# A kernel whose order comes from a list of jobs: GpSimd jobs tied to the vector job ahead of them, new durations in the list, and transposed rows offered later

## The chip, the cores and the metric

The kernel runs on one core of a Trainium2 chip, as one program. The metric is the device time of one execution in microseconds (us), median of three runs. The engines are TensorE (PE; its weight loads PEld), VectorE (DVE), ScalarE (ACT), GpSimd (POOL) and SyncE (SP, which here issues the DMAs). Each runs its own instructions in the order in which the program lists them, and waits for the others through semaphores.

## The reference

Attention over 4 batches, 12 heads, 448 positions and head size 64, in float32, and then two feed-forward layers on the 1792 rows of 768:

```
q_n, k_n = rmsnorm(q, g_q), rmsnorm(k, g_k)        # x / sqrt(mean(x*x) + 1e-6) * g
scores = q_n @ k_n.T / 8;  scores -= rowmax(scores)
attn = exp(scores);  attn /= (rowsum(attn) + 1e-9)
x = heads_joined(attn @ v)                         # [1792, 768]
x = square(relu(x @ w_in)) @ w_out                 # 768 -> 2048 -> 768
g = x @ w_gate
out = (silu(g) * (x @ w_val)) @ w_out2             # 768 -> 1536 -> 768
```

## The kernel before

Attention works on 24 pairs of heads, g = 0 to 23, six to a batch. A pair has 7 tiles of scores (`PT`), 128 rows by 448 each. For a tile PE multiplies (`sc`), DVE takes the negated row maximum and scales it by the query's norm (`maxima`: `sc`, `m`), ACT takes the exponential with the sum of each row (`ring`, `sum`), PE turns the result by four transposes (`pt`), ACT copies that out of PSUM (`turned_p`); when seven are there, PE multiplies with the values (`o`). Products in full precision are made of high and low parts (`kst`, `kst_lo` and so on): the high part is a cast on ACT or DVE, the low part a subtraction on GpSimd or DVE.

The norms come beside that. Squares of the keys and queries (`nat`) are made on ACT or GpSimd, DVE sums them (`ss`), and `rsqrt` makes the inverse root by three Newton steps: for the first pairs all of it on DVE, later the three steps on GpSimd, each a job of four small instructions (`rst`, `rms`). The result for the keys lies in `stage`. `transposed` turns it on PE (`rows` from `stage`), ACT copies it out (`rkr`), and for the first five pairs PE spreads it over the partitions (`rk`) for the scaling of the keys (`kq`). The sums of the exponentials go the same way: `norms` takes their reciprocal on DVE (`sum`), `transposed` turns them (`rows` from `sum`), ACT copies them (`zr`), PE spreads them (`zb`, first five pairs), and they scale `o` into `ox`, from which the input `x` of the first layer is made.

PE has other work only once the list says that the 35th exponential is done (`LEND`): from then on products of the first layer (`h_a`, `ya`, line 325) stand between those of attention. Ahead of it small transposes (`warm`) fill PE's first 20 us. After attention only the two layers are left.

No one writes the order by hand. Each step is a generator that yields jobs, such as `yield {"A": 467, "W": 300}, f`: f may run on ACT for 467 ns or on DVE for 300 ns. "P" is PE, "G" GpSimd, "V" a vector job, and "W" a vector job that takes part in the port described below. A clock of the list's own runs through these durations while the program is built; `dispatch` takes, for each engine that is free on that clock, the ready job of lowest rank and emits its instructions. An engine other than the first named takes a job only when the first is behind by more than a spare time. So the durations decide which engine takes a job and in which order everything stands; the chip then runs each engine's list in that order, with waits only for data. `port` is a time up to which, on the list's clock, neither a GpSimd job nor a "W" job may start: the list never lets them overlap, but nothing holds the chip to that.

Of the kernel before, what the change touches and what calls it, by code (L numbers as in the profile page):

```python
# [14 lines left out]
ALU = mybir.AluOpType  # L15
# [37 lines left out]
X_AT = 3  # L53
X_FLIGHT = 3
PE_SLACK = 500
JOIN_FROM = 6
OUT_ORDER = [2, 3, 4, 5, 0, 1]
DEC_FIRST = 14
# [20 lines left out]
def attention_two_ffn_kernel(  # L79
# [19 lines left out]
    nc = tc.nc  # L99
    PSUM = bass.MemoryType.PSUM  # L100

    def as_f32(ap):
        return ap.bitcast(F32)
# [66 lines left out]
                heapq.heappush(timers, (clock[0] + p, serial[0], t, None))  # L170
            return

    port = [0.0]

    def meant(job):
        e = next(iter(job[1][0]))
# [15 lines left out]
    def dispatch(e):  # L192
        queues[e] = [job for job in queues[e] if not job[3]]
        if not queues[e] or free_at[e] > clock[0]:
            return False
        q = [job for job in queues[e] if e == meant(job) or late(job) > cost(job, e) + spare[e]]
        if port[0] > clock[0]:
            q = [job for job in q if not ported(job, e)]
        if not q:
            return False  # L200
        job = min(q, key=lambda job: (job[0].rank, job[2]))
        job[3] = True
        t, p, _, _ = job
        p[1](engines[e])
        done = free_at[e] = clock[0] + cost(job, e)
        if ported(job, e):
            port[0] = done
        if e == "S":
            dma_free[0] = max(dma_free[0], clock[0] + 1100) + p[2] / DMA_RATE
            done = dma_free[0] + 900  # L210
        else:
            done += p[2] if len(p) > 2 else settle[e]
        heapq.heappush(timers, (done, job[2], t, e))
        return True
# [46 lines left out]
    def load_weights(items):  # L261

        hilo, parts = {}, {}

        def chunk(key, place, c, raw_at):
            name, f = key  # L270
            late = f"{name}{f}_{c}"
            src = w_tiles[name][f] if name in w_tiles else w_rows[name][bass.ts(f, 128), :]
            src = src.bitcast(I32).rearrange("p (n two) -> p n two", two=2)
            raw = raw_at[0].tile([128, WC, 2], I32, tag=raw_at[1], name=f"raw_{late}")
            yield from dma(lambda e: e.dma_start(out=raw, in_=src[:, bass.ts(c, WC), :]), 8 * WC * 128)
            yield lambda: was and not leading
            a_at = was.pop(0)
            a = a_at[0].tile([128, WC], F32, tag=a_at[1], name=f"wa_{late}")
            yield {"A": 413, "W": 269}, lambda e: (
                e.activation(out=a, in_=raw[:, :, 1].bitcast(F32), func=ACTF.Copy, scale=2.0 ** -112)  # L280
                if e is nc.scalar
                else e.tensor_scalar(
                    out=a, in0=raw[:, :, 1].bitcast(F32), scalar1=2.0 ** -112, scalar2=None, op0=ALU.mult
                )
            )
            yield lambda: wts
            t_at = wts.pop(0)
            t = t_at[0].tile([128, WC], F32, tag=t_at[1], name=f"wt_{late}")
            ai, ti = a.bitcast(I32), t.bitcast(I32)
            yield {"W": 269}, lambda e: e.tensor_scalar(  # L290
                out=ti, in0=raw[:, :, 0].bitcast(U32), scalar1=2.0 ** -29, scalar2=7.0, op0=ALU.mult, op1=ALU.min
            )
            raws.append(raw_at)
            yield {"W": 469}, lambda e: e.scalar_tensor_tensor(
                out=ti, in0=ai, scalar=SIGN_BIT, in1=ti, op0=ALU.bitwise_and, op1=ALU.bitwise_or
            )
            yield {"W": 469}, lambda e: e.scalar_tensor_tensor(
                out=ti, in0=ai, scalar=3, in1=ti, op0=ALU.logical_shift_left, op1=ALU.bitwise_or
            )
            was.append(a_at)  # L300
            if c == 0:
                yield lambda: place or free
                pool, hi_tag, lo_tag = placed[key] = place or free.pop(0)
                hilo[key] = tuple(
                    pool.tile([128, DM], F32R, tag=tag, name=f"{part}_{name}{f}")
                    for part, tag in (("hi", hi_tag), ("lo", lo_tag))
                )
                parts[key] = 0
            yield lambda: key in hilo
            hi, lo = (x[:, bass.ts(c, WC)] for x in hilo[key])  # L310
            yield {"A": 413, "W": 269}, lambda e: copy(e, hi, t)
            yield {"W": 469, "G": 956}, lambda e: e.tensor_tensor(out=lo, in0=t, in1=as_f32(hi), op=ALU.subtract)
            wts.append(t_at)
            parts[key] += 1
            if parts[key] == DM // WC:
                wt[key] = hilo[key]

        for key, place, rank in items:
            for c in range(DM // WC):
                yield lambda: raws  # L320
                spawn(chunk(key, place, c, raws.pop(0)), rank + c / 10)
# [123 lines left out]
    def rsqrt(y, ss, t, ends, fused):  # L445

        def begin(e):
            e.tensor_scalar(out=ss, in0=ss, scalar1=1.0 / D, scalar2=EPS_RMS, op0=ALU.mult, op1=ALU.add)
            e.tensor_scalar(
                out=y.bitcast(I32), in0=ss.bitcast(I32), scalar1=-0.5, scalar2=RSQRT_MAGIC, op0=ALU.mult, op1=ALU.add  # L450
            )

        def step(e, to):
            e.tensor_tensor(out=t, in0=y, in1=y, op=ALU.mult)
            if fused:
                e.scalar_tensor_tensor(out=t, in0=t, scalar=-0.5, in1=ss, op0=ALU.mult, op1=ALU.mult)
            else:
                e.tensor_tensor(out=t, in0=t, in1=ss, op=ALU.mult)
                e.tensor_scalar(out=t, in0=t, scalar1=-0.5, scalar2=1.5, op0=ALU.mult, op1=ALU.add)
            for dst, part in to:  # L460
                a, b = (t, y) if part is None else (t[:, part], y[:, part])
                if fused:
                    e.scalar_tensor_tensor(out=dst, in0=a, scalar=1.5, in1=b, op0=ALU.add, op1=ALU.mult)
                else:
                    e.tensor_tensor(out=dst, in0=a, in1=b, op=ALU.mult)

        if fused:
            def all_steps(e):
                begin(e)
                for i in range(3):  # L470
                    step(e, ends if i == 2 else [(y, None)])

            yield {"W": 170 * (10 + len(ends))}, all_steps
            return
        yield {"W": 300}, begin
        for i in range(3):
            yield {"G": 900}, lambda e: step(e, ends if i == 2 else [(y, None)])

    stat, halves = {}, {}
    sum_wide, stage = (  # L480
# [10 lines left out]
    def row_sums(g, w):  # L491

        b, p = divmod(g, PB)
        yield lambda: nat_free
        where = nat_free.pop(0)
        x = tile_at(where, [128, PT * D], F32, f"nat{g}_{w}")
        src = (k_n, q_n)[w][b][:, bass.ts(p, PT * D)]
        yield from dma(lambda e: e.dma_start(out=x, in_=src), 128 * PT * D * 4)
        yield {"A": 467} if g == 0 else {"G": 1091, "A": 467}, lambda e: (
            e.activation(out=x, in_=x, func=ACTF.Square) if e is nc.scalar  # L500
            else e.tensor_tensor(out=x, in0=x, in1=x, op=ALU.mult)
        )
        rows = x.rearrange("p (t d) -> p t d", d=D)
        if g or w:
            yield lambda: (1 if g and Q_HOLD > 1 else 0) in summed
        yield {"V": 535}, lambda e: e.tensor_reduce(out=stat["ss", b][:, w, p], in_=rows, axis=AX.X, op=ALU.add)  # L506
        if where[0] is not xp:
            nat_free.append(where)
        halves[g] = halves.get(g, 0) + 1
# [45 lines left out]
    def spread(rows, parts, name):  # L555
# [9 lines left out]
                    start=True, stop=True,  # L565
                )

        yield {"P": 1100}, broadcast, 0
        return ps, where

    def spread_k(g, rows, r):
# [34 lines left out]

    def transposed(src, dst):

        yield lambda: t_banks
        where = t_banks.pop(0)  # L610
        pt = tile_at(where, [128, 512], F32, "rows")
# [50 lines left out]
    def split(g, x, name, w):  # L662
        yield lambda: g < 2 or scored[0] >= PT * (g - 1)
        hi = ap.tile([128, w], F32R, tag=f"{name}{g % 2}", name=f"{name}{g}")
        lo = ap.tile([128, w], F32R, tag=f"{name}{g % 2}_lo", name=f"{name}_lo{g}")
        yield {"A": 467, "W": 300}, lambda e: copy(e, hi, x)
        yield {"G": 1106, "W": 535}, lambda e: e.tensor_tensor(out=lo, in0=x, in1=as_f32(hi), op=ALU.subtract)
        return [hi, lo]

    def release_kq(g):  # L670
# [4 lines left out]
    def prep_k(g, kr, rk, rk_at):  # L675

        yield lambda: gained
        e = yield {"W": 596, "A": 467}, lambda e: (
            e.activation(out=kr, in_=kr, func=ACTF.Copy, scale=gqk[:, 0:1]) if e is nc.scalar
            else e.scalar_tensor_tensor(out=kr, in0=kr, scalar=gqk[:, 0:1], in1=rk, op0=ALU.mult, op1=ALU.mult)  # L680
        )
# [70 lines left out]
    def softmax(g, tiles, parts, tops, where):  # L752
# [17 lines left out]
                )  # L770
                at += each

        yield {"V": 215 * len(tops) + n * 467}, maxima
        if g not in sums:
            yield lambda: g in sums or sum_free
            if g not in sums:
# [19 lines left out]
    def norms(g):  # L796
# [3 lines left out]
            e.tensor_scalar(out=z, in0=z, scalar1=EPS_SUM, scalar2=None, op0=ALU.add)  # L800
            e.reciprocal(z, z)

        yield {"V": 240}, inverse
        yield lambda: zr_free
        zr_at = zr_free.pop(0)
        rows = tile_at(zr_at, [128, 128], F32, f"zr{g}")
# [506 lines left out]
```

## Time and profile before

| | |
|---|---|
| median of 3 runs | 1297.2 us (1293.56 to 1297.56) |
| profiled execution | 1290.19 us, its span 1288.4 us |
| PE busy | 1258.1 us (98%) |
| DVE, ACT, POOL busy | 667.6, 573.0, 156.3 us |
| granted clock, mean of the span | 0.999 |

The rows further down are of the one profiled execution. A row of the wait view gives the idle time of an engine before a line's instructions and what ended it; one of the timeline the start, the length, and in brackets the idle time just before. PE counts as busy from a product's start to its modelled end, so its idle time is what it waits, not all that it could gain.

### The profile page before, as it was taken

The numbers are of one execution on the slowest core, as the hardware profiler recorded it, in microseconds if no ns is written. First come the engines' busy times: TensorE is split into PE (matmuls) and PEld (weight loads), VectorE is DVE, ScalarE is ACT, GpSimd is POOL, SyncE is SP. The second block draws the span as 40 slices with busy tenths as digits, with TensorE's granted clock in tenths as the row PEclk, the third lists the DMA queues.
The fourth block names the chain that finished last, engine by engine and source line by source line (L and its number), as shares of the span: only waits on it lengthen the run. The fifth ranks groups of instructions, "written<-read, shape, count | busy, mean of one in ns | idle before, by whom it ended". The sixth has DMA issues, their size and how long they took to land.

```text
span 1288.4 us, 18441 instructions
## 1 busy us (share of the span) xinstructions
PE 1258.1 (98%) x6710; PEld 1079.9 (84%) x6710; DVE 667.6 (52%) x1357; ACT 573.0 (44%) x1257; POOL 156.3 (12%) x263
## 2 busy tenths in 40 slices
PE   8878999999999999999999999999999999999998
PEld 6555777777777999999999999999999999999998
DVE  7999964554543997249333783212148712213122
ACT  6898986776775656135322442212126411202110
POOL 4443633443210000000000000000000000000000
PEclk9999999999999999999999999999999999999999
DMA  6567564344313667137343563010127500203021
GB/s 210 150 200 197 161 189 124 110 123 134 93 43 104 209 192 254 52 114 226 113 129 129 172 206 126 21 65 7 37 63 232 154 1 1 86 1 129 1 86 43
DMA packets 85469, 151.02 MB, mean 117 GB/s; under 512 B 14641, under 2 KB 64962, under 8 KB 85378
## 3 DMA queue, kind: packets, MB, share of 16 engines
q1 hardware_dynamic: 85378, 149.84, 37.0%
q8 instruction: 53, 0.87, 0.3%
q14 instruction: 38, 0.31, 0.1%
HBM read 120.75 MB, written 29.04 MB: 116 GB/s over the span
## 4 chain that ended last, share of the span: by engine, by line
PE 83%; DVE 7%; ACT 4%; DMA 2%; issue 2%; POOL 1%; SPq 0%; DVEq 0%; ACTq 0%; POOLq 0%
PE y L325 27%; PE h_v L325 14%; PE h_g L325 14%; PE h L325 12%; PE ya L325 4%; PE o L878 3%; PE pt L845 3%; PE h_a L325 3%; PE sc L739 3%; DVE sc L767 2%; ACT ring L781 2%; ACT turned_p L218 1%; DVE ss L506 1%; DMA raw_out<-in_w_out_dram 1%; PE h_lead L325 1%
## 5 line engine op out<-in xcount | busy, mean ns | idle before, releaser
L325 PE MATMUL h_v<-x,hi_v 128*128 128x448 f32 x576 | 164.4, 366 | 0.0
L325 PE MATMUL h_g<-x,hi_g 128*128 128x448 f32 x576 | 164.3, 366 | 0.0
L325 PE MATMUL y<-s,hi_o 128*128 128x448 f32 x576 | 164.1, 366 | 0.0
L325 PE MATMUL y<-s,hi_out 128*128 128x448 f32 x552 | 157.2, 366 | 0.0
L325 PE MATMUL h<-x,hi_in 128*128 128x448 f32 x516 | 147.4, 367 | 0.0
L378 DVE TENSOR_TENSOR sig<-h_g,sig 128x448 f32<-128x448 f32 x48 | 29.9, 623 | 216.7 <-ACT sig L377 216.7
L781 ACT ACTIVATE ring<-sc,m,rms 128x448 f32<-128x448 f32 x168 | 124.0, 741 | 29.8 <-PE pt L845 20.2
L377 ACT ACTIVATE sig<-h_g 128x448 f32<-128x448 f32 x48 | 26.1, 544 | 219.3 <-PE h_g L325 219.2
L325 PEld LDWEIGHTS h_v<-x,hi_v 128*128 128x128 f32 x576 | 108.2, 188 | 9.3
L325 PEld LDWEIGHTS h_g<-x,hi_g 128*128 128x128 f32 x576 | 108.2, 188 | 9.2
L325 PEld LDWEIGHTS y<-s,hi_o 128*128 128x128 f32 x576 | 108.1, 188 | 9.3
L767 DVE TENSOR_REDUCE sc<-sc 128x2 f32<-128x896 f32 (+1 forms) x96 | 93.8, 977 | 38.0 <-PE sc L739 37.6
L325 PEld LDWEIGHTS y<-s,hi_out 128*128 128x128 f32 x552 | 103.5, 188 | 8.8
L845 PE MATMUL pt<-ident,ring 128*128 128x128 f32 x672 | 101.8, 276 | 9.2 <-ACT turned_p L218 2.9
L845 PEld LDWEIGHTS pt<-ident,ring 128*128 128x128 f32 x672 | 78.8, 140 | 33.5 <-ACT turned_p L218 6.6
L325 PE MATMUL h_v<-x,lo_v 128*128 128x448 f32 x288 | 105.4, 366 | 0.0
L325 PE MATMUL y<-s,lo_o 128*128 128x448 f32 x288 | 105.4, 366 | 0.0
L325 PE MATMUL h_g<-x,lo_g 128*128 128x448 f32 x288 | 105.4, 366 | 0.0
L325 PEld LDWEIGHTS h<-x,hi_in 128*128 128x128 f32 x516 | 96.9, 188 | 8.6
L218 ACT COPY turned_p<-pt 128x512 f32<-128x512 f32 x165 | 97.0, 596 | 11.0 <-PE pt L845 10.8
L325 PE MATMUL y<-s,lo_out 128*128 128x448 f32 x276 | 100.8, 365 | 0.0
L325 PE MATMUL h<-x,lo_in 128*128 128x448 f32 x258 | 94.5, 366 | 0.0
(155 smaller groups left out, 2135.8 us busy)
## 6 DMA issues: line engine op xcount, KB each, us to landing
raw_in<-in_w_in_dram SPq DMA_DIRECT2D x32, 384.0 KB, 3.3
raw_out<-in_w_out_dram SPq DMA_DIRECT2D x32, 384.0 KB, 3.5
kq<-in_kq_p_dram SPq DMA_DIRECT2D x23, 480.0 KB, 3.6
xr<-x2d SPq DMA_DIRECT2D x42, 224.0 KB, 4.8
raw_g<-in_w_gate_dram SPq DMA_DIRECT2D x24, 384.0 KB, 3.1
raw_v<-in_w_val_dram SPq DMA_DIRECT2D x24, 384.0 KB, 3.6
raw_o<-in_w_out_dram SPq DMA_DIRECT2D x24, 384.0 KB, 4.0
xr<-x1d SPq DMA_DIRECT2D x36, 224.0 KB, 4.5
```

Source lines behind the costliest of these rows:

```text
L218: e.copy(out, src)
L325: return {"P": 203}, lambda e: e.matmul(ps, lhsT=w, rhs=x, start=first, stop=last), 0
L377: yield {"A": 424}, lambda e: e.activation(out=t, in_=pg, func=ACTF.Sigmoid)
L378: yield {"V": 535}, lambda e: e.tensor_tensor(out=t, in0=pg, in1=t, op=ALU.mult)
L506: yield {"V": 535}, lambda e: e.tensor_reduce(out=stat["ss", b][:, w, p], in_=rows, axis=AX.X, op=ALU.add)
L739: e.matmul(parts[t][:, :S], lhsT=q[a][d, bass.ts(i % 4, 128)], rhs=k[c][d], start=(p == 0), stop=(p == len(passes) - 1),)
L767: e.tensor_reduce(out=top, in_=sc, axis=AX.X, op=ALU.max, negate=True)
L781: yield {"A": 704}, lambda e: e.activation(out=probs(at + t), in_=parts[t][:, :S], func=ACTF.Exp, bias=m[:, t:t + 1], scale=rq[:, i:i + 1] ...
L845: e.transpose(ps[:, bass.ts(j, 128)], p[:, bass.ds(min(128 * j, S - 128), 128)], ident)
L878: e.matmul(o[64 * h:64 * h + 64], lhsT=v[:, 4 * h + j], rhs=turned_p[:, 2 * j + h], start=(j == 0), stop=(j == 3),)
```

## The change

Three edits. First, `dispatch` remembers the last instruction of the last "W" job that it emitted, and gives the first instruction of every GpSimd job a wait for it; a vector job gets no wait for a GpSimd job. Second, eleven durations of the list are set anew. Third, `transposed` waits 800 ns on the list's clock (`ROWS_SLACK`) before it offers its transpose to PE, once a first exponential is done. No arithmetic changes.

```diff
+ROWS_SLACK = 800
...
+    port, port_last = [0.0], []
+    behind = mybir.DependencyInfo(mybir.DependencyClass.Sync, mybir.DependencyReason.DATA)
+
+    def traced():
+        return nc.cur_bb.bb.instructions
...
+        before = len(traced())
         p[1](engines[e])
+        if ported(job, e):
+            if e == "V":
+                port_last[:] = [traced()[-1]]
+            elif port_last:
+                first = next(i for i in traced()[before:] if i.engine == engines["G"].engine)
+                tc.add_manual_dep(first, port_last[0].name, behind, reason="port")
         done = free_at[e] = clock[0] + cost(job, e)
...
-            yield {"W": 170 * (10 + len(ends))}, all_steps
+            yield {"W": 190 * (10 + len(ends))}, all_steps
...
-            yield {"G": 900}, lambda e: step(e, ends if i == 2 else [(y, None)])
+            yield {"G": 1265 + 165 * (i == 2)}, lambda e: step(e, ends if i == 2 else [(y, None)])
...
-        yield {"A": 467} if g == 0 else {"G": 1091, "A": 467}, lambda e: (
+        yield {"A": 467} if g == 0 else {"G": 900, "A": 467}, lambda e: (
...
-        yield {"P": 1100}, broadcast, 0
+        yield {"P": 950}, broadcast, 0
...
     def transposed(src, dst):
 
+        if expd[0]:
+            yield ROWS_SLACK
         yield lambda: t_banks
...
-        e = yield {"W": 596, "A": 467}, lambda e: (
+        e = yield {"W": 596, "A": 560}, lambda e: (
...
-        yield {"V": 215 * len(tops) + n * 467}, maxima
+        yield {"V": 265 * len(tops) + n * 467}, maxima
...
-        yield {"V": 240}, inverse
+        yield {"V": 320}, inverse
```

The others are the scaled copy of a weight on ACT (`wa`, 413 to 455) and the two parts of a 512-column tile (467 to 515, 300 to 335, 1106 to 1245 and 535 to 605).

How the built programs stand, at three places. On GpSimd, the first chain of Newton steps (`rst`, `rms` are its tiles, `kst_lo` the low part of the keys of pair 1), before and then after the change; in brackets the semaphores that a row waits for:

```order
L667 TENSOR_TENSOR kst_lo1_486<-kq1_336,kst1_485 128x448 [waits Activation_49]
L454 TENSOR_TENSOR rst0_283<-rms0_284 128x2x14 [waits DVE_49]
L458 TENSOR_TENSOR rst0_283<-rst0_283,ss0_282 128x2x14 [waits Pool_49]
L459 TENSOR_SCALAR rst0_283<-rst0_283 128x2x14 [waits Pool_49]
L465 TENSOR_TENSOR rms0_284<-rst0_283,rms0_284 128x2x14 [waits Pool_49]
L454 TENSOR_TENSOR rst0_283<-rms0_284 128x2x14 [waits Pool_49]
```

```order
L681 TENSOR_TENSOR kst_lo1_490<-kq1_336,kst1_489 128x448 [waits Activation_49]
L466 TENSOR_TENSOR rst0_283<-rms0_284 128x2x14 [waits DVE_49]
L470 TENSOR_TENSOR rst0_283<-rst0_283,ss0_282 128x2x14 [waits Pool_49]
L471 TENSOR_SCALAR rst0_283<-rst0_283 128x2x14 [waits Pool_49]
L477 TENSOR_TENSOR rms0_284<-rst0_283,rms0_284 128x2x14 [waits Pool_49]
L466 TENSOR_TENSOR rst0_283<-rms0_284 128x2x14 [waits DVE_49,Pool_49]
```

The second step now waits for a vector instruction too; before it waited for its own engine alone. Over the whole program 26 rows of GpSimd waited for DVE, and 65 do now.

On GpSimd, some pairs later, around the input `x` of pair 5 and the low parts for pairs 8 and 9, before and after:

```order
L501 TENSOR_TENSOR nat11_1_1632<-nat11_1_1632 128x448 [waits DMAHW5_49,DVE_49]
L924 TENSOR_TENSOR x1_5_1747<-ox5_1743,x1_5_1747 128x448 [waits Activation_49]
L667 TENSOR_TENSOR kst_lo8_1764<-kq8_1369,kst8_1763 128x448 [waits Activation_49]
L667 TENSOR_TENSOR qst_lo9_1789<-kq9_1503,qst9_1788 128x512 [waits DMAHW7_49,PE_49,Activation_49]
L501 TENSOR_TENSOR nat12_0_1787<-nat12_0_1787 128x448 [waits DMAHW6_49]
```

```order
L513 TENSOR_TENSOR nat11_1_1635<-nat11_1_1635 128x448 [waits DMAHW3_49,Pool_49]
L938 TENSOR_TENSOR x1_5_1754<-ox5_1743,x1_5_1754 128x448 [waits DVE_49,Activation_49]
L681 TENSOR_TENSOR kst_lo8_1742<-kq8_1347,kst8_1741 128x448 [waits Activation_49]
L324 TENSOR_TENSOR lo_out2_1777<-wt_out2_0_1691,hi_out2_1776 128x384 [waits Activation_49]
L466 TENSOR_TENSOR rst1_700<-rms1_701 128x2x14 [waits DVE_49]
```

The part of `x` waits for DVE now, a low part of a weight (`lo_out`) has come over from DVE, and the low part for pair 9 stands further down.

On PE, the end of pair 1 (`o1` is its product with the values, `sc8` the first scores of pair 2), before and after:

```order
L739 MATMUL sc9_793<-kst2_665,qst_lo2_593 128x448 x2
L612 MATMUL rows_807<-ident_205,sum1_275 128x128
L845 MATMUL pt13_794<-ident_205,ring_266 128x128 x4
L739 MATMUL sc10_811<-kst2_665,qst2_592 128x448 x2
L739 MATMUL sc10_811<-kst_lo2_666,qst2_592 128x448 x2
L739 MATMUL sc10_811<-kst2_665,qst_lo2_593 128x448 x2
L563 MATMUL zb1_834<-zr1_806,pick_222 64x128 x6
L563 MATMUL zb1_834<-zr1_806,pick_222 64x64 x2
L612 MATMUL rows_847<-ident_205,stage1_277 128x128
L878 MATMUL o1_848<-turned_p_267,v1_269 64x448 x8
```

```order
L859 MATMUL pt12_767<-ident_205,ring_266 128x128 x4
L859 MATMUL pt13_778<-ident_205,ring_266 128x128 x4
L626 MATMUL rows_787<-ident_205,sum1_275 128x128
L575 MATMUL zb1_798<-zr1_783,pick_222 64x128 x6
L575 MATMUL zb1_798<-zr1_783,pick_222 64x64 x2
L892 MATMUL o1_810<-turned_p_267,v1_269 64x448 x8
L753 MATMUL sc8_832<-kst2_756,qst2_577 128x448
L753 MATMUL sc8_832<-kst_lo2_757,qst2_577 128x448
L753 MATMUL sc8_832<-kst2_756,qst_lo2_578 128x448
```

The turned sums stood ahead of the last transposes of their pair and stand behind them now; three groups of scores of pair 2 (`sc8` to `sc10`) stood ahead of `o1` and stand behind it. PE's products are the same but for `warm`, 64 before and 71 now.

## Rows read from the trace of the kernel before

**Rows 1.** The page: busy time of the engines and its share of the span.
```profile
PE 1258.1 (98%) x6710; PEld 1079.9 (84%) x6710; DVE 667.6 (52%) x1357; ACT 573.0 (44%) x1257; POOL 156.3 (12%) x263
```

**Rows 2.** Busy time by stretch: PE, PEld, DVE, ACT, POOL, granted clock, DMA share, GB/s.
```profile
25.00:50.00 25.00, 20.88 (x171) 13.36 (x172) 23.21 (x49) 21.84 (x55) 12.71 (x27) 0.93 0.66 201
50.00:75.00 25.00, 19.68 (x169) 13.64 (x167) 22.75 (x51) 21.07 (x52) 11.07 (x10) 1.00 0.50 155
75.00:100.00 25.00, 22.25 (x159) 14.49 (x156) 23.41 (x51) 24.19 (x59) 12.30 (x16) 1.00 0.63 185
100.00:150.00 50.00, 44.50 (x262) 30.36 (x260) 45.31 (x93) 41.23 (x98) 21.62 (x38) 1.00 0.65 180
```

**Rows 3.** Waits of PE, 12 to 150 us: total, times, longest.
```profile
PE rows L612 <- DVE sum L801: 4.0, 3, 1.6
...
PE h_a L325 <- DVE r_a L362: 2.0, 1, 2.0
...
PE rows L612 <- POOL stage L465: 0.9, 1, 0.9
```

**Rows 4.** Waits of ACT, 12 to 94 us.
```profile
ACT rkr L613 <- PE rows L612: 4.2, 3, 3.0
ACT ring L781 <- DVE m L768: 4.2, 4, 2.5
ACT zr L613 <- PE rows L612: 2.9, 3, 1.2
```

**Rows 5.** Timeline of PE: start, length, instruction, idle time before.
```profile
9.52 1.75 PE L1009 MATMUL warm<-ident 128*128 128x128 f32 x14
...
27.40 0.33 PE L612 MATMUL rows<-ident,stage 128*128 128x128 f32 x1 [0.90 <-POOL stage L465]
...
36.72 0.45 PE L739 MATMUL sc<-kst,qst 128*128 128x448 f32 x1
...
42.66 0.30 PE L612 MATMUL rows<-ident,sum 128*128 128x128 f32 x1 [1.61 <-DVE sum L801]
...
94.00 0.45 PE L325 MATMUL h_a<-x,hi_in 128*128 128x448 f32 x1
```

**Rows 6.** Timeline of ACT: two exponentials that follow each other, numbers 12 and 13.
```profile
32.24 0.72 ACT L781 ACTIVATE ring<-sc,m,rms 128x448 f32<-128x448 f32 x1
...
38.10 0.74 ACT L781 ACTIVATE ring<-sc,m,rms 128x448 f32<-128x448 f32 x1
```

**Rows 7.** Timeline of DVE: some vector instructions that took long, and one neighbour.
```profile
18.58 1.38 DVE L290 TENSOR_SCALAR wt_in<-raw_in 128x384 int32<-128x384 uint32 x2
...
59.23 0.17 DVE L463 SCALAR_TENSOR_TENSOR stage<-rst,rms 128x14 f32<-128x14 f32 x1
59.32 1.11 DVE L463 SCALAR_TENSOR_TENSOR rms<-rst,rms 128x14 f32<-128x14 f32 x1
...
118.47 1.51 DVE L297 SCALAR_TENSOR_TENSOR wt_out<-wa_out,wt_out 128x384 int32<-128x384 int32 x1
...
123.05 1.48 DVE L220 CAST kst<-kq 128x448 fp32r<-128x448 f32 x1
124.44 1.28 DVE L294 SCALAR_TENSOR_TENSOR wt_out<-wa_out,wt_out 128x384 int32<-128x384 int32 x1
...
412.08 1.21 DVE L312 TENSOR_TENSOR lo_in<-wt_in,hi_in 128x384 fp32r<-128x384 f32 x1 [0.73 <-ACT hi_in L218]
```

**Rows 8.** Lines of DVE: ns shortest/median/longest, first and last start, form.
```profile
L297 DVE SCALAR_TENSOR_TENSOR wt_out<-wa_out,wt_out x32: 505/549/1511, 101.5 to 495.3; 128x384 int32<-128x384 int32 x32
...
L220 DVE CAST kst<-kq x3: 379/471/1477, 69.2 to 123.0; 128x448 fp32r<-128x448 f32 x3
...
L767 DVE TENSOR_REDUCE sc<-sc x96: 619/1090/1103, 15.5 to 390.9; 128x2 f32<-128x896 f32 x72, 128x1 f32<-128x448 f32 x24
```

**Rows 9.** Groups of POOL, 12 to 400 us: busy, mean ns, idle before and releasers.
```profile
L667 POOL TENSOR_TENSOR qst_lo<-kq,qst 128x512 fp32r<-128x512 f32 x22 | 28.3, 1287 | 74.9 <-ACT qst L218 72.0 <-DVE m L768 2.0 <-DVE qst L220 0.9
```

**Rows 10.** Groups of ACT, 12 to 94 us.
```profile
L500 ACT ACTIVATE nat<-nat 128x448 f32<-128x448 f32 x5 | 2.9, 578 | 0.0
```

More of the change, by code (lines that the diff above doesn't have):

```diff
@@ L171, in resume @@
             return
-    port = [0.0]
+    port, port_last = [0.0], []
+    behind = mybir.DependencyInfo(mybir.DependencyClass.Sync, mybir.DependencyReason.DATA)
+    def traced():
+        return nc.cur_bb.bb.instructions
     def meant(job):
@@ L278, in chunk @@
             a = a_at[0].tile([128, WC], F32, tag=a_at[1], name=f"wa_{late}")
-            yield {"A": 413, "W": 269}, lambda e: (
+            yield {"A": 455, "W": 269}, lambda e: (
                 e.activation(out=a, in_=raw[:, :, 1].bitcast(F32), func=ACTF.Copy, scale=2.0 ** -112)
@@ L665, in split @@
         lo = ap.tile([128, w], F32R, tag=f"{name}{g % 2}_lo", name=f"{name}_lo{g}")
-        yield {"A": 467, "W": 300}, lambda e: copy(e, hi, x)
-        yield {"G": 1106, "W": 535}, lambda e: e.tensor_tensor(out=lo, in0=x, in1=as_f32(hi), op=ALU.subtract)
+        yield {"A": 467 if w == S else 515, "W": 300 if w == S else 335}, lambda e: copy(e, hi, x)
+        yield {"G": 1106 if w == S else 1245, "W": 535 if w == S else 605}, lambda e: e.tensor_tensor(out=lo, in0=x, in1=as_f32(hi), op=ALU.subtract)
         return [hi, lo]
```

## The prediction

> **What bounds the kernel now.** I read the page first, then busy time by stretch, then the waits of PE and ACT, then the timelines. PE is busy for 98% of the span [rows 1]; all that it waits for is about 30 us. By stretch, 17.7 us of that lie between 25 and 150 us (4.12 + 5.32 + 2.75 + 5.50) [rows 2]. The two layers behind attention have PE full, and nothing in the change adds or takes a product there. So the change is worth what it does to the first 150 us, and above all to the stretch ahead of 94.0 us, where PE gets its first product of the first layer [rows 5]: before that point PE has nothing with which to fill a wait, so a delay of attention is a delay of the end.
>
> In that stretch PE is not the bound. From 25 to 100 us DVE is busy for 69.4 of 75 us and ACT for 67.1 [rows 2]. Two engines at 93 and 89%, tied to each other through PE's list, make a loop: a pause of one becomes a pause of the next. The reader can see it in one kind of wait. PE waited for the reciprocal of the sums three times, 4.0 us together, and once 0.9 us for the keys' norms from GpSimd [rows 3]; since PE's list is in order, all behind `rows` waited too. Behind it ACT sat idle for the copies of those rows, 2.9 us for `zr` and 4.2 us for `rkr` [rows 4], 3.0 us of the latter in a single first wait that belongs to the start. So 4.1 us of ACT's idle time hang on turned rows that were offered when their input was not there yet.
>
> **GpSimd behind the vector job.** Vector instructions of usual length 0.17 to 0.55 us took 1.1 to 1.5 us where GpSimd had started just before [rows 7, 8]. Taking each against the usual one of its line and form, I count 26 such between the first row at 18.58 and the last at 412.08 [rows 7], 18.3 us lost, 0.70 us each. I then looked where the two stand in the list. In 22 cases (14.6 us) the vector job stands behind the GpSimd job: GpSimd was where the list wanted it, or late, and the wait that is added does nothing for these. In 4 cases GpSimd had run ahead of a vector job that stands before it, and these the wait takes away: at 59.32, 118.47, 123.05 and 124.44 [rows 7], by the usual 0.17, 0.55, 0.38 and 0.55 us [rows 7, 8] a loss of 0.94 + 0.96 + 1.10 + 0.73 = 3.7 us of DVE. How much reaches PE: the last two lie ahead of `r_a`, for which PE then waited 2.0 us [rows 3]; their 1.83 us I take as gained. The first two lie ahead of row maxima, with PE and ACT busy on other tiles; they count between 0 and 1.9, I take 0. So -1.8, bounds 0 and -3.7.
>
> The wait has a price. Rows that wait for DVE go from 26 to 65. Queued behind a waiting GpSimd job are the Newton steps (then `stage`, `rows`, `rk` and the next keys), squares (then DVE's sums) and low parts (then PE's second and third pass). Against a price speaks that GpSimd usually comes late by itself: its low parts of the queries sat idle for ACT's cast for 72.0 us in 22 jobs [rows 9]. Where it binds, it costs up to a vector job, 0.55 us [rows 8], for each further step of a Newton chain, two in a chain; PE's only wait on `stage` in this stretch was 0.9 us [rows 3]. I take +0.8, bounds 0 and +3.
>
> The trace shows one more thing: the 96 row maxima, which read PSUM, never took long, 1.103 us at most beside a median of 1.090 [rows 8]. A rule of the Trainium skill agrees with that and speaks against the change: "SBUF — State Buffer", section "Who interferes with whom", says that a row reduction never contends, and that of the others whichever starts first, VectorE or GpSimd, holds the shared port for its whole instruction. By the rows the sum goes as above; by the rule alone a wait on one side only turns the order round, more vector jobs would start second, and the sum would be that of the last rival below.
>
> **Rows offered later.** In the new order the turned sums stand behind the last transposes of their pair. By then a group of transposes, and mostly one of scores, has gone by. What goes is at most PE's 4.9 us (4.0 + 0.9) [rows 3] and ACT's 4.1 us [rows 4]. What is late next: `zr`, `zb` and `ox`, which have the rest of a pair as cover. Since DVE is near its bound, part of a gap returns as a wait for the next maxima (ACT already waits 4.2 us for `m` [rows 4]). I take -3.0 of 4.1; bounds 0 and -4.9.
>
> **The clock.** From 25 to 50 us the granted clock was 0.93 [rows 2]: PE ran for a few microseconds at the lower of its levels, 1.2 for 2.4 GHz. That is 0.07 x 25 = 1.75 us, right behind the wait of 1.61 us at 42.66 [rows 5]. If that wait goes, this may go; another gap may bring it back. I take half, -0.9; bounds 0 and -1.75.
>
> **New durations.** They move jobs. Up to the 35th exponential ACT has 125 instructions for 123: casts of keys and queries come to it from DVE, squares go to GpSimd. Two more at about 0.58 us [rows 10] are +1.2; I take +1.0, since ACT has 11% to spare. DVE has one fewer, which I cost at nothing. Seven more `warm` products at 1.75/14 us [rows 5] are 0.9 us of PE; they stand where PE waits for the first scores on DVE, whose chain covers them, so 0, and 0.9 if that cover is gone. The largest move is at pair 2: its keys' rows stood ahead of `o0` and now stand behind it, and its first scores, at 36.72 us before [rows 5], come after `o1`. It could delay the exponentials by up to 5 us. Cover: between the exponentials at 32.24 and 38.10 [rows 6] ACT already ran 5 us of other jobs without a pause, and these are still there. So 0, and +5 without that cover.
>
> **The sum.** -1.8 + 0.8 - 3.0 - 0.9 + 1.0 = -3.9 us. The profiled execution took 1290.2 us, so 1286.3 in its terms. The median of the runs shown is 1297.2, 7 us above it; the runs differ by 4.0 us among themselves, which is 0.3%, about what a measurement of this kernel can tell from no change. I put the difference on the median: **1293.3 us**. Adding the bounds of the wait, its price, the rows, the clock and the durations gives from -10 to +10, but they will not all fall one way.
>
> **Rivals.**
> *Nothing that shows.* The wait is a wait in name only, because GpSimd is later than the vector job anyway [rows 9], and the gaps of PE that close ahead of `rows` open ahead of `sc` and `pt` because ACT and DVE have no more than 7 to 11% to give. Within 1.5 us of before: about 1297. Against it: ACT's waits for rows are real idle time of one of the two bounding engines.
> *More than the sum.* Durations nearer to the truth close gaps all along, half of PE's 17.7 us between 25 and 150 us [rows 2]: -8.9, 1288.3. For it: the list gave a Newton step 900 ns where it gives 1265 now. Against it: the engines' load stays as it was.
> *Slower: vector jobs blocked behind GpSimd.* GpSimd is let go the moment a vector job ends, and with DVE at 93% the next vector job is at the door. Each that finds GpSimd started loses 0.70 us. If 20 more are blocked, DVE loses 14 us; half of it reaching PE is +7.0, the rows' gain halves to -1.5, the clock gives nothing, with -1.8 and +1.0 as above: +4.7, about 1302. It decides from some 18 more on, about half of the 39 new waits. For it: 22 of 26 blocked jobs stood behind GpSimd already. Against it: the list now holds the port longer for chains of Newton steps, and maxima, which stand between most vector jobs, are not blocked.
>
> **How the numbers follow.** The sum 0.50, of which half lies beyond 0.3% (3.9 us) and half within; nothing that shows 0.16; more than the sum 0.16; slower 0.18, nearly all beyond 0.3%. Faster 0.25 + 0.16 = 0.41, with a little from the sum's own far side 0.43; slower 0.17; the rest, 0.40, no difference. The range reaches from some 4 us below the third case, 1284, to the fourth, 1302. The likeliest case alone: 1290 to 1297.
>
> **What the profile after would show.** PE's waits of `rows` for `sum` gone or under 1 us together, and ACT's for `zr` with them; first product `h_a` some 2 to 4 us ahead of 94.0; no vector instruction blocked by a GpSimd job that stands behind it in the list, and no fewer of the others; PE idle from 25 to 150 us near 13 us. I would be wrong if the first scores of pair 2 leave ACT idle around 35 to 45 us, if blocked vector instructions rise well above 26, or if `stage` comes so late that PE waits for it.

## The result, and the profile after

The changed kernel took 1284.1 us (median of 5 runs, 1282.4 to 1284.5) beside 1294.7 us for the kernel before, run beside it (5 runs, 1292.9 to 1297.6): ratio 0.991, 95% interval 0.9892 to 0.9929. That is 10.7 us faster where 3.9 were forecast. The profiled execution took 1282.4 us (span 1280.6), 7.8 us below the one of before, which was among the fastest of its kernel.

Busy time of the changed kernel, from the page, answering to [rows 1]. PE worked 1.1 us longer, so its idle time in the span fell by 8.9 us.

```profile
PE 1259.2 (98%) x6717; PEld 1086.3 (85%) x6717; DVE 656.0 (51%) x1349; ACT 570.5 (45%) x1252; POOL 161.0 (13%) x274
```

The same stretches as in [rows 2]: PE, PEld, DVE, ACT, POOL, granted clock, DMA share, GB/s.

```profile
25.00:50.00 25.00, 20.43 (x166) 12.55 (x165) 21.05 (x43) 21.88 (x53) 14.10 (x27) 0.95 0.70 223
50.00:75.00 25.00, 22.25 (x157) 15.49 (x157) 22.71 (x54) 22.48 (x56) 9.72 (x9) 0.92 0.45 140
75.00:100.00 25.00, 23.57 (x174) 17.91 (x170) 22.16 (x49) 24.13 (x60) 14.04 (x23) 1.00 0.73 221
100.00:150.00 50.00, 47.77 (x283) 34.63 (x284) 47.57 (x101) 44.57 (x106) 19.53 (x36) 1.00 0.66 190
```

From 25 to 150 us PE was idle for 4.57 + 2.75 + 1.43 + 2.23 = 11.0 us, beside 17.7 before. All the stretches gained but the first. In this execution the clock did not get better than in the one of before: 0.95 and 0.92 from 25 to 75 us, where only one stretch of before was below 1.

Waits of PE (12 to 150 us) and then of ACT (12 to 94 us) in the changed kernel, as in [rows 3] and [rows 4].

```profile
PE sc L753 <- ACT ring L795: 3.9, 4, 2.3
PE rows L626 <- ACT turned_p L230: 1.1, 2, 0.8
...
PE rows L626 <- DVE rms L475: 0.2, 1, 0.2
```

```profile
ACT rkr L627 <- PE rows L626: 2.9, 2, 2.4
ACT hi_in L230 <- DVE wt_in L309: 2.2, 2, 1.6
...
ACT ring L795 <- DVE m L782: 0.8, 2, 0.4
```

PE's 4.0 us of waits for `sum` and ACT's 2.9 us for `zr` are gone. PE's waits of `sc` for `ring` are not much longer in all, but before they came in small pieces:

```profile
PE sc L739 <- ACT ring L781: 3.2, 7, 0.5
```

Now one of them is 2.3 us long, where the scores of pair 2 come later. The timeline of PE and that of ACT show it: `sc` of pair 2 starts at 44.14 (36.72 before, [rows 5]), and between the two exponentials at 36.30 and 47.27, which follow each other, ACT has time to spare.

```profile
44.14 0.47 PE L753 MATMUL sc<-kst,qst 128*128 128x448 f32 x1
...
92.37 0.57 PE L337 MATMUL h_a<-x,hi_in 128*128 128x448 f32 x2
```

```profile
36.30 0.73 ACT L795 ACTIVATE ring<-sc,m,rms 128x448 f32<-128x448 f32 x1
...
43.60 0.51 ACT L230 CAST hi_in<-wt_in 128x384 fp32r<-128x384 f32 x1 [1.62 <-DVE wt_in L309]
...
47.27 0.71 ACT L795 ACTIVATE ring<-sc,m,rms 128x448 f32<-128x448 f32 x1
```

By the first product `h_a`, at 92.37 for 94.00, attention has caught up and is 1.6 us ahead. Most of the gain comes behind it: from 100 to 150 us alone PE's idle time fell from 5.50 us [rows 2] to 2.23.

### The profile page after: what moved, and what is told of

Read it like the earlier page. It is cut to its first block, busy times and chain, and to the rows that moved or that the text cites. A ratio compares the mean times of both kernels' runs of the same rounds, so it can differ in the third digit from the quotient of the medians.

```text
span 1280.6 us, 18475 instructions
## 1 busy us (share of the span) xinstructions
PE 1259.2 (98%) x6717; PEld 1086.3 (85%) x6717; DVE 656.0 (51%) x1349; ACT 570.5 (45%) x1252; POOL 161.0 (13%) x274
## 4 chain that ended last, share of the span: by engine, by line
PE 87%; DVE 6%; DMA 3%; ACT 2%; issue 1%; SPq 0%; DVEq 0%; ACTq 0%; POOLq 0%
PE y L337 25%; PE h_v L337 14%; PE h_g L337 14%; PE h L337 11%; PE ya L337 5%; PE o L892 4%; PE h_a L337 4%; PE pt L859 4%; PE sc L753 4%; DMA nat<-in_q_n_dram 1%; ACT ring L795 1%; DVE sc L781 1%; DMA zb<-zd 1%; ACT turned_p L230 1%; PE h_lead L337 1%
```

## The experiments

Each median stands beside the kernel before in the same session (1292.8 to 1293.6 us). "Blocked" is counted as in the prediction: vector instructions from 12 to 430 us well over the usual time of their line and form, with GpSimd in its own instruction when they start.

### One edit at a time, and two at a time

The wait alone is this edit of the kernel before:

```
         p[1](engines[e])
+        if ported(job, e):
+            if e == "V":
+                port_last[:] = [traced()[-1]]
+            elif port_last:
+                first = next(i for i in traced()[before:] if i.engine == engines["G"].engine)
+                tc.add_manual_dep(first, port_last[0].name, behind, reason="port")
```

> The list of before, with the wait of each GpSimd job for the vector job ahead of it, and nothing else. If the wait makes the gain: -6 to -10 us, and fewer vector instructions blocked by GpSimd. If the gain is the new order: within 3 us of before. If one-sided waits only turn the order round (the lock rule): +2 to +6 us and more than 26 blocked vector instructions.

Rows later alone is `ROWS_SLACK = 800` with its two lines in `transposed`; durations alone is the table of the change without the other two edits.

> Before, with transposed rows offered 800 ns later, old durations, no wait. By the prediction's term: -3 to -5 us, PE's and ACT's waits for rows gone. If the new durations make the gain: within 2 us of before. If any new order is a new deal of the cards: anything from -6 to +6 us, with other waits changed than those for rows.

> Before, with the new durations alone. By the prediction's term: 0 to +2 us. If durations nearer to the truth make the gain: -6 to -10 us, PE idle between 25 and 150 us well under 13 us.

> The changed kernel without the wait: the same list, new durations, rows later. If the wait makes the gain: -4 us or less of it is left. If the order makes it: -8 to -11 us. By the prediction's terms: 1 us worse than the changed kernel, so about -9.7.

> The changed kernel without the later rows: the wait and the new durations. If the wait does it whatever the list: -10 to -12 us. If the three edits add up (-11.5, -7.1 and -8.3 us were measured one at a time): -17 us or more.

> The changed kernel with the durations of before: the wait and the later rows. If the wait does it whatever the list: -10 to -12 us. If the edits add up: -17 us or more. If the later rows close PE's waits as the prediction has it, 3 us better than the wait alone: -14 us.

Measured:

| kernel | median us | ratio, 95% interval | granted clock, median of the runs |
|---|---|---|---|
| before, in these sessions | 1292.8 and 1293.3 | | 0.993 |
| wait alone | 1281.8 | 0.9912 (0.9898 to 0.9926) | 0.998 |
| rows later alone | 1286.2 | 0.9940 (0.9927 to 0.9953) | 0.999 |
| durations alone | 1285.0 | 0.9934 (0.9919 to 0.9949) | 0.997 |
| rows and durations, no wait | 1287.3 | 0.9949 (0.9936 to 0.9961) | 0.9965 |
| wait and durations | 1282.0 | 0.9912 (0.9890 to 0.9934) | 0.997 |
| wait and rows | 1281.1 | 0.9898 (0.9875 to 0.9920) | 0.9975 |
| all three (the change; before beside it 1294.7) | 1284.1 | 0.9910 (0.9892 to 0.9929) | 0.996 |

The wait alone wins all that the change wins. Each of the other two wins 7 to 8 us alone, both without the wait no more, and nothing that can be measured beside the wait. No version with the wait is clearly better than another. A part of every gain goes with the clock, which is higher in all of these kernels than before; how much is said under the clock below.

### Which vector instructions the wait sets free

The kernel with the wait alone has the same list as before, so the two traces can be laid beside each other. The first place: DVE and POOL of the kernel before, two pairs into attention.

```profile
69.48 1.42 DVE L282 TENSOR_SCALAR wa_in<-raw_in 128x384 f32<-128x384 f32 x1
70.83 1.35 DVE L667 TENSOR_TENSOR kst_lo<-kq,kst 128x448 fp32r<-128x448 f32 x1
```

```profile
69.40 1.29 POOL L667 TENSOR_TENSOR qst_lo<-kq,qst 128x512 fp32r<-128x512 f32 x1 [0.90 <-DVE qst L220]
70.65 1.04 POOL L501 TENSOR_TENSOR nat<-nat 128x448 f32<-128x448 f32 x1
```

And the same four instructions with the wait alone.

```profile
65.41 0.35 DVE L293 TENSOR_SCALAR wa_in<-raw_in 128x384 f32<-128x384 f32 x1
65.68 0.61 DVE L678 TENSOR_TENSOR kst_lo<-kq,kst 128x448 fp32r<-128x448 f32 x1
```

```profile
66.44 1.29 POOL L678 TENSOR_TENSOR qst_lo<-kq,qst 128x512 fp32r<-128x512 f32 x1 [2.00 <-DVE sum L811]
67.68 0.95 POOL L512 TENSOR_TENSOR nat<-nat 128x448 f32<-128x448 f32 x1
```

Before, GpSimd took `qst_lo` as soon as its input was there, 0.08 us ahead of `wa_in`, which took 1.42 us for 0.35; then `nat` caught `kst_lo`. With the wait, `qst_lo` starts 0.15 us after the end of `kst_lo` (65.68 + 0.61), the vector job that it now waits for; the profile names `sum`, which ended about then too. So `wa_in` and `kst_lo` both stand ahead of `qst_lo` in the list, and GpSimd had overtaken them. For the second of the two the prediction had it the other way round.

The error was in the source. I had taken the order across engines from where the instructions stand in the built program. But an instruction that waits for nothing of another engine may stand there on either side of the other's, so that place says nothing of the list. The targets of the new waits do: a vector instruction stands ahead in the list if it is at or ahead of the instruction for which the GpSimd job waits. Read so, the blocked instructions of before are 27, with `wa_in` above, which my count lacked because its line ran only once on DVE. In 12 of them, 10.0 us, GpSimd had run ahead of the list; the other 15, 9.3 us, stand behind that instruction. The prediction had 4 and 22. Three of the 15 are `sum` (84.38, 183.47 and 199.16 us, 1.9 us together), which the list counts as "V" and not to the port (`inverse` in the change's diff), so that it may itself put a GpSimd job beside it; for these "behind" says only that the wait does not cover them.

```profile
84.38 1.10 DVE L800 TENSOR_SCALAR sum<-sum 128x7 f32<-128x7 f32 x1
```

By the same reading (in the other kernels without lines that ran only once):

| kernel | blocked, vector job ahead in the list | blocked, vector job behind |
|---|---|---|
| before | 12, 10.0 us | 15, 9.3 us |
| wait alone | 0 | 19, 11.9 us |
| the change | 0 | 20, 10.7 us |
| rows later alone | 10, 8.3 us | 14, 6.4 us |
| durations alone | 7, 4.3 us | 18, 7.4 us |
| rows and durations, no wait | 10, 8.2 us | 13, 7.7 us |

Durations alone has two more ahead in the list before 12 us, at 6.42 and 7.57 us, 1.5 us together.

Two runs then asked whether these twelve carry the gain, or a later GpSimd as such. One gives the wait to the twelve GpSimd jobs alone, the other to all the rest (`g_jobs` counts the jobs of GpSimd; the edit stands against the wait alone, and the other run has `not in AHEAD`):

```
+AHEAD = (2, 13, 20, 21, 23, 24, 31, 40, 41, 42, 43, 60)
...
-            elif port_last:
+            else:
+                g_jobs[0] += 1
+            if e == "G" and port_last and g_jobs[0] in AHEAD:
```

> The kernel before, with the wait on 12 of its GpSimd jobs alone: those of which the first wait alone showed that the list puts the blocked vector job ahead of them (the jobs that held the port at 18.58, 39.86, 57.73, 59.32, 69.48, 70.83, 86.79, 116.96, 118.47, 123.05, 124.44 and 159.61 us of the trace of before; 10.0 us lost in these 12). Theory A, these twelve lost instructions are what the wait wins: about 10 us off, 1282 to 1285. Theory B, the wait wins by a later start of GpSimd as a whole, whichever jobs have it: a part of 11.5 us by the number of waits, 12 of some 40, so 3 to 4 us off, 1289 to 1290.

> The kernel before, with the wait on all GpSimd jobs but those 12. Theory A: as the kernel before within 3 us, 1290 to 1296, the twelve instructions still blocked where GpSimd comes at the same moments. Theory B: two thirds of the gain of the wait, 7 to 8 us off, 1285 to 1286.

With the twelve alone: 1283.5 us, 0.9923 (0.9903 to 0.9943). With all others: 1291.9 us, 0.9992 (0.9976 to 1.0007), no change. DVE with the twelve alone, at the places of [rows 7]:

```profile
65.64 0.35 DVE L296 TENSOR_SCALAR wa_in<-raw_in 128x384 f32<-128x384 f32 x1
65.91 0.61 DVE L681 TENSOR_TENSOR kst_lo<-kq,kst 128x448 fp32r<-128x448 f32 x1
...
112.67 0.56 DVE L311 SCALAR_TENSOR_TENSOR wt_out<-wa_out,wt_out 128x384 int32<-128x384 int32 x1
...
116.30 0.39 DVE L234 CAST kst<-kq 128x448 fp32r<-128x448 f32 x1
116.60 0.55 DVE L308 SCALAR_TENSOR_TENSOR wt_out<-wa_out,wt_out 128x384 int32<-128x384 int32 x1
```

And with all others:

```profile
69.46 1.44 DVE L296 TENSOR_SCALAR wa_in<-raw_in 128x384 f32<-128x384 f32 x1
70.83 1.35 DVE L681 TENSOR_TENSOR kst_lo<-kq,kst 128x448 fp32r<-128x448 f32 x1
...
118.22 1.50 DVE L311 SCALAR_TENSOR_TENSOR wt_out<-wa_out,wt_out 128x384 int32<-128x384 int32 x1
...
122.79 1.47 DVE L234 CAST kst<-kq 128x448 fp32r<-128x448 f32 x1
124.18 1.28 DVE L308 SCALAR_TENSOR_TENSOR wt_out<-wa_out,wt_out 128x384 int32<-128x384 int32 x1
```

The reader is to see the lengths: 1.44, 1.35, 1.50, 1.47 and 1.28 us against 0.35, 0.61, 0.56, 0.39 and 0.55 for the same five instructions. The first theory of these two expectations holds. The second is out: all other waits together win nothing.

### The wait turned round, and on both sides

Here each vector job of the port waits for the GpSimd job ahead of it; once without and once with the wait of GpSimd. The edit stands against the wait alone; the first of the two leaves out the wait of GpSimd.

```
             if e == "V":
+                if pool_last:
+                    first = next(i for i in traced()[before:] if i.engine == engines["V"].engine)
+                    tc.add_manual_dep(first, pool_last[0].name, behind, reason="port")
+                    pool_last.clear()
                 port_last[:] = [traced()[-1]]
+            if e == "G":
+                pool_last[:] = [traced()[-1]]
```

> The list of before, with the wait turned round: each vector job of the port waits for the GpSimd job ahead of it, GpSimd waits for nothing more. If any order on the port helps: -5 to -10 us. If what helps is that a GpSimd job steps back until the vector queue has moved on, this gives nothing or costs: 0 to +6 us, and blocked vector instructions stay, as waits of DVE for GpSimd.

> The list of before with waits on both sides: GpSimd for the vector job ahead of it, and each vector job of the port for the GpSimd job ahead of it. Blocked vector instructions become waits of DVE. If order on the port is the thing: as good as the wait of GpSimd alone or better, -11 to -14 us. If GpSimd's stepping back is the thing, holding DVE too loses it: -4 to +4 us.

Turned round: 1299.5 us, 1.0039 (1.0023 to 1.0054), slower. Both sides: 1292.1 us, 0.9998 (0.9988 to 1.0007). Turned round, 16 instructions ahead in the list are still blocked (13.1 us) and 3 behind (2.1 us). With both, 2 are left in all (0.7 us): the list's order is kept, and nothing is won. The waits of DVE for GpSimd, 12 to 400 us, with both:

```profile
DVE ss L523 <- POOL nat L518: 4.5, 5, 1.6
DVE lo_out L329 <- POOL rms L482: 3.0, 2, 1.5
DVE kq L697 <- POOL rms L482: 2.6, 2, 1.3
DVE sa L383 <- POOL rms L482: 2.4, 2, 1.5
...
DVE sa L383 <- POOL nat L518: 0.2, 1, 0.2
```

But for the first, which needs the data, these 23 rows hold 28.0 us that the kernel before does not have. Vector jobs that are held until GpSimd is done lose more together than they lost when blocked (19.3 us by the table above).

### Waiting for any vector job, and another list

GpSimd waits for the last vector job of whatever kind, maxima included: `if e == "V" or ported(job, e):`, once with the list of before and once with the rows later. And a list that was to be dealt anew for no purpose: `settle` of DVE 135 for 125 ns.

> The list of before, GpSimd waiting for the last vector job of any kind ahead of it in the list, not of the port alone. In most of the 20 blocked cases that are left with the wait, GpSimd started beside a vector instruction that is not of the port (a maximum, a sum) with a job of the port next in the queue. If GpSimd's stepping back is the thing: fewer than 10 blocked, and 1 to 4 us better than the wait alone, -12.5 to -15.5 us. If GpSimd then comes too late for PE: -4 to -9 us, and PE waits for its low parts or for the norms.

> The same wait with the later rows and the durations of before. By the stepping back: better than the wait with later rows (-12 us by its run), -13 to -17 us. By the lateness of GpSimd: -5 to -10 us.

> Before, with one small number of the list changed that has nothing to do with the port (the time that a vector result takes to settle, 125 to 135 ns), no wait. If the gain of the two edits of the list alone is only a new deal of a bad list: -3 to -8 us here too. If the durations and the rows are what gained: within 2 us of before.

Any vector job: 1295.8 us, 1.0023 (1.0012 to 1.0033); with the rows later 1290.9, 0.9984 (0.9974 to 0.9994). New deal: 1293.2, 0.9996 (0.9982 to 1.0010). Both ranges that I had given for each of the first two are missed. I had expected fewer blocked instructions of the longer wait, and it has more, 30 (18.1 us), all behind GpSimd in the list. One place, POOL and DVE with the wait for any vector job:

```profile
62.74 1.14 POOL L678 TENSOR_TENSOR kst_lo<-kq,kst 128x448 fp32r<-128x448 f32 x1 [3.94 <-DVE m L779]
63.84 1.26 POOL L694 TENSOR_TENSOR kq<-kq,rkb 128x448 f32<-128x448 f32 x1
```

```profile
63.73 1.59 DVE L301 TENSOR_SCALAR wt_in<-raw_in 128x384 int32<-128x384 uint32 x2
```

And the same place in the kernel with the wait alone:

```profile
56.47 1.14 POOL L678 TENSOR_TENSOR kst_lo<-kq,kst 128x448 fp32r<-128x448 f32 x1 [3.40 <-ACT turned_p L229]
57.56 1.13 POOL L694 TENSOR_TENSOR kq<-kq,rkb 128x448 f32<-128x448 f32 x1
```

```profile
57.45 1.10 DVE L778 TENSOR_REDUCE sc<-sc 128x2 f32<-128x896 f32 x1
...
58.66 0.64 DVE L301 TENSOR_SCALAR wt_in<-raw_in 128x384 int32<-128x384 uint32 x2
```

With the wait of the change, both GpSimd jobs run beside two maxima, which they do not disturb, and are done when `wt_in` comes. Held until the first maximum and its `m` have gone by, they end a maximum later and the second meets `wt_in`: 1.59 us for 0.64. The new deal is none where it matters. The traces of it and of before have the same operations and tiles in the same order on PE, ACT, DVE and GpSimd up to 300 us, but for one `warm` ahead of 10 us; the next that differs is at 303 us on ACT. So it does not tell whether any other list would win as the rows and the durations do. It tells something else, which I had overlooked: what two executions of one order can differ by. These are its stretches and its first `h_a`, which comes 4.25 us behind the 94.00 of [rows 5].

```profile
25.00:50.00 25.00, 21.18 (x163) 13.64 (x165) 22.33 (x46) 21.20 (x53) 12.16 (x24) 0.86 0.62 189
50.00:75.00 25.00, 18.94 (x148) 12.88 (x145) 22.62 (x48) 19.39 (x48) 11.68 (x10) 0.94 0.49 153
75.00:100.00 25.00, 23.27 (x150) 14.85 (x149) 22.11 (x46) 22.45 (x53) 8.76 (x8) 0.85 0.53 168
```

```profile
98.25 0.45 PE L325 MATMUL h_a<-x,hi_in 128*128 128x448 f32 x1
```

The granted clock was 0.86, 0.94 and 0.85 in these stretches, and 0.93, 1.00 and 1.00 in [rows 2].

## Why the prediction was wrong

**What bounds the kernel** held: PE's idle time fell in the stretch that was named, from 17.7 to 11.0 us between 25 and 150 us, where I looked for about 13. The first `h_a` is 1.6 us ahead, where 2 to 4 were forecast.

**The wait** is the step that failed. The prediction says: "In 22 cases (14.6 us) the vector job stands behind the GpSimd job: GpSimd was where the list wanted it, or late, and the wait that is added does nothing for these." By the waits' own targets 15 of 27 stand behind, and 12 are such as the wait takes away. What was said of the profile after came true by this reading: none blocked that stands ahead in the list, and no fewer of the others (20 for 15). Of the four that I had, I let 1.83 of 3.7 us reach PE. In fact most of the twelve did. Seven of them, up to 86.79 us, cost 5.6 us, and with the wait alone the first `h_a` comes 5.1 us ahead of the 94.00 of [rows 5]:

```profile
88.92 0.45 PE L336 MATMUL h_a<-x,hi_in 128*128 128x448 f32 x1
```

So the cover that I gave the first two, "PE and ACT busy on other tiles", does not hold while DVE is at 93% and each maximum waits in its queue. The term was -1.0 with its price; it measured -11.5 with all the waits and -10.1 with the twelve, beside 10.0 us lost. That the last two agree so well is partly luck, since some 4 us of either gain go with the clock by the estimate below. Without that part the wait is worth some 7 us, and by the profiled executions of before and of the wait alone, both at a clock of 0.999, 10.8. The bounds, 0 and -3.7, came from the same count and were too narrow for that reason.

**The price of the wait** was at the low end: with the wait alone PE's waits for `stage` went from 0.9 to 1.1 us (below), DVE's for GpSimd's squares, 12 to 400 us, from 6.9 to 6.1.

**Rows offered later.** -3.0, with a bound of -4.9, was too small for the edit alone (-7.1 us, of which some 5 go with the clock by the estimate below; its profiled execution, also at 0.999, is 3.1 us below the one of before) and too large for the change, where it adds nothing that can be measured. What goes was named rightly: the waits for `sum`. But these have a cause that the wait takes away as well. PE's waits for `rows` with the wait alone, where the rows are not offered later:

```profile
PE rows L623 <- POOL stage L476: 1.1, 2, 0.9
PE rows L623 <- DVE sum L812: 0.6, 1, 0.6
```

4.0 us of [rows 3] are 0.6. With the twelve waits alone they are 0.8, with all the others 3.9:

```profile
PE rows L626 <- DVE sum L815: 0.8, 2, 0.6
```

```profile
PE rows L626 <- DVE sum L815: 3.9, 2, 2.3
```

The sums came late because DVE was behind; with DVE in time there was little for the later offer to save. I counted one delay in two terms.

**The durations.** +1.0 had the wrong sign: -8.3 alone. I priced two more instructions on ACT and not what a new list does to the meetings of DVE and GpSimd: its blocked instructions ahead in the list cost 4.3 us from 12 us on, where those of before cost 10.0, and PE's waits for `sum` are gone here too. Some 3.5 us of the 8.3 go with the clock. The late scores of pair 2, +5 without cover, came as feared, with 1.62 us of idle ACT in one piece, and were made up by 92 us; by what, no run shows.

**The clock.** Between the two profiled executions -0.9 did not come: by the rows above, 0.05 x 25 + 0.08 x 25 = 3.3 us were lost from 25 to 75 us, for 1.75 before. The drop now lies about the new gap at pair 2; that the one made the other was not tried. But the term was worked out from one execution, and that one was not like its kernel. Its mean granted clock was 0.999. In the 76 runs of the kernel before beside the experiments the clock was 0.989 to 0.997, median 0.993, and they are longer where it is lower: 1295.5 us on average at 0.992 (9 runs), 1290.2 at 0.997 (3 runs). A straight line through the 76 gives 0.9 us for 0.001. The new deal above shows the same in a trace: one order, a lower clock, and the first `h_a` 4.25 us later. The changed kernel ran at 0.996 to 0.998, so by this estimate some 2.5 us of its 10.7 go with the clock, where the bound was 1.75; of the wait alone 4.3, of the rows alone 5.2. The 7 us between the profiled execution and the median of before, which the prediction took for the runs' own spread, may be the clock too. The kernels in the table above have a higher clock than before, and each lacks PE's 4.0 us of waits for `sum` but for 0.6 at most; that fewer of PE's pauses keep the clock up is likely, but no run tries it alone.

**Rivals.** "More than the sum" was nearest, 1288.3, but for another reason than the durations alone. "Nothing that shows" is out. "Slower" (whose sum left out the price of 0.8) did not come: blocked instructions fell from 27 to 20. A rule stood behind it: by the Trainium skill, "SBUF — State Buffer", section "Who interferes with whom", whoever issues first holds the shared port for the whole instruction. As far as it goes the traces agree: holding GpSimd freed the vector side, and with the wait turned round 16 were left blocked. What I drew from it, that a wait on one side only turns the order round, was too strong: those behind rose from 15 to 19 (+2.6 us), against twelve that went.

**What stays open.** How much of each gain is the clock is an estimate. Without the wait, rows and durations together win less (6.0 us) than their parts would; with it they win nothing. Their aims overlap with the wait's in the two counts shown, late sums and instructions overtaken by GpSimd, but no run takes one of the two away alone, so how much each holds of the 7 and 8 us is argued, not shown. Nor is it shown that these two edits win by what they aim at: no list that differs for no purpose in the first 150 us was run.

## What to carry to other kernels

When a list plans two engines around a shared port, find out from real dependences which of two jobs the list puts first; the place of instructions of different engines in the built program does not tell. Price each vector instruction that was overtaken at most of its loss if the vector engine is near its bound, and look for the same delay in later waits before giving these a term of their own. Let the less busy engine wait, and only for jobs that it can disturb: waits on the busy side cost as much as the blocking, and a longer wait than needed moves the meeting to the next job. Before pricing the clock from one trace, look at the granted clock of many runs: here the trace at hand was better than any of 76 others.

## What the runs showed of the hardware

A blocked vector instruction ends only after GpSimd's has: `wa_in` at 69.48 ended at 70.90, and `qst_lo` at 70.69. The 27 of the kernel before lost 19.3 us, 0.7 us each, while `qst_lo` took 1.29 us with a blocked neighbour (69.40, before) and without one (66.44, with the wait). Row maxima ran beside GpSimd at 1.10 us, as without it; `sum`, which the list leaves outside the port as it does the maxima, did not: 1.10 us for 0.17 at 84.38. One order of instructions took 4.25 us longer to its first `h_a` at granted clocks of 0.86 to 0.94 than at 0.93 to 1.00. What I had not expected is how little a released GpSimd instruction costs the queue: it starts 0.15 us after the vector instruction that it waits for, and by then the next vector instruction has often begun and keeps its usual time, as `sum` did at 66.22:

```profile
66.22 0.16 DVE L811 TENSOR_SCALAR sum<-sum 128x7 f32<-128x7 f32 x1
```
